# A fused attention, mixture-of-experts and cos-gated MLP kernel: first decay rows through TensorE, a merged score visit, V products in two visits, another last block

## The chip, the cores and the metric

The kernel runs on one core of one Trainium2 chip. The metric is the device time of one execution in microseconds (us); lower is better. Names used below: PE is TensorE (PEld its weight loads), DVE is VectorE, ACT is ScalarE, POOL is GpSimd, SP is SyncE, which here only issues DMAs.

## The reference

Three stages follow one another. With 4 batches, 8 heads, 576 positions and 64 channels a head:

```
s_pos  = max(s, 0);  cum = cumsum(s_pos)
scores = q k^T / 8 + min(-(cum_i - cum_j), 0), causal
attn   = softmax(scores) (row sum + 1e-9);  out = attn @ v          # -> x, 2304 x 512
logits = (x/|x|) (e/|e|)^T / tau;  each token goes to its best of 8 experts
y      = gate * (relu(x @ w1[e]) @ w2[e])                           # 512 -> 1024 -> 512
h      = y @ w_in;  out = (h * cos(h)) @ w_out                      # 512 -> 2048 -> 512
```

## The kernel before

**Attention** (`attention`, lines 67 to 442) works through 16 pairs of heads. A pair's 576 queries are cut into five tiles: tile 4 is the last 64 queries of both heads together, tiles 3, 2, 1 and 0 are 128 queries each and see 512, 384, 256 and 128 keys. `steps` (L205) is the list of all (pair, tile), in the order 4, 3, 2, 1, 0. For one step:

- `emit_s` writes the scores q k^T into two PSUM banks of the pool `ps_s` (four banks), by fp32 products of 64 by 64 (L218 for tile 4, L225 for the others); a tile other than 4 has one bank for each head.
- `emit_m` adds the causal mask to the diagonal block by a bf16 product with the identity `idb` (L235, L238).
- `emit_x` lets DVE add the decay row `c_t` and take the row minimum in one instruction (L255, with a small read-out `mx`), and ACT take the exponential and the row sum (L260).
- `emit_t` transposes the result on PE (L271, L277, banks of `ps_t`) and copies it to `PT` on DVE (tiles 1 and 2) or ACT.
- `av` multiplies by V (L293) once all tiles of a pair are there: 256 query columns first, then 320 (the last pair the other way round).

The loop (L421 to L439) runs at step n: mask of n+3, transposes of n, one turn of the waiting tasks, reductions and exponentials of n+2, scores of n+4, another turn of the tasks. A task is a generator and gives up its turn at each `yield`; `av`, `setup` and, for each batch of four pairs, `rows` and `route` (output rows, router logits, positions, scatter) are such tasks. The order on PE and on SP is the order of this text; DVE, ACT and POOL are ordered by the scheduler of the framework.

`c_t` of a pair holds the running sums of two heads, each spread over 128 partitions, and a third row set for tile 4. The sums are scanned on DVE (L120), written to device memory (`cumd`, L121) and read back with one row for all partitions (L98, L100). `load`, `load_c` and `load_v` of pair p+2 are issued on SP at pair p's first step; `q`, `k` and `c` have three buffers each. `setup` also issues eight writes of zeros over `xr` (L202), 768 KB each.

**Experts** (`moe1`) and **MLP** (`moe2`, lines 812 to 904) follow. The MLP cuts 2304 tokens into blocks of 256 (block 0) and four times 512, and the hidden 2048 into 16 chunks whose weights pass through a ring of six. A window is a run of up to four chunks for one block; its products accumulate in PSUM (`facc`) and are added to `oacc` at its end (L885); where a window ends at chunk 15 the finished rows are scattered to the output by POOL (L887), one instruction for each 128 tokens. `first` (L830) sets after how many chunks a block's first window ends; windows are sorted by end and start.

Of the kernel before, what the change touches and what calls it, by code (L numbers as in the profile page):

```python
# [66 lines left out]
def attention(g, qd, kd, vd, sd, ied, embt, tau, ident, maskd, trid):  # L67
    tc, nc, const, dram, xr = g.tc, g.nc, g.const, g.dram, g.xr
    with ExitStack() as st:
# [25 lines left out]
        def load_c(p, eng=nc.sync):  # L95

            c_t = ct[p] = ld.tile([128, 3, S], F32, tag="c", name="c_t")
            eng.dma_start(out=c_t[:, 0:2], in_=cumd[2 * p:2 * p + 2].unsqueeze(0).to_broadcast([128, 2, S]))  # L98
            for h in range(2):
                eng.dma_start(out=c_t[64 * h:64 * h + 64, 2], in_=cumd[2 * p + h].unsqueeze(0).to_broadcast([64, S]))  # L100
# [7 lines left out]
        mk_f = one.tile([128, 192], F32, name="mk_f")  # L108
        mk_b = one.tile([128, 192], BF16, name="mk_b")
# [97 lines left out]
        sc, px, rs, ot = {}, {}, {}, {}  # L207

        def emit_s(n):
            p, i = steps[n]  # L210
            q0, q1 = QT[i]
            q_t, k_t = qt[p], kt[p]
            if i == 4:
# [6 lines left out]
            else:  # L220
                ts = [ps_s.tile([128, 512], F32, tag="s", name="s_ps") for h in range(2)]
                for u in range(2):
                    for h, t in enumerate(ts):
                        a = q0 + 64 * u
                        nc.tensor.matmul(out=t[64 * u:64 * u + 64, 0:q1], lhsT=q_t[64 * h:64 * h + 64, a:a + 64], rhs=k_t[64 * h:64 * h + 64, 0, 0:q1],  # L225
                                         start=True, stop=False)
                sc[n] = ts

        def emit_m(n):

            p, i = steps[n]
            q0, q1 = QT[i]
            if i == 4:
                t, c0, c1 = sc[n][1]
                nc.tensor.matmul(out=t[:, 224:288], lhsT=idb, rhs=mk_b[:, 128:192], start=False, stop=True)  # L235
            else:
                for t in sc[n]:
                    nc.tensor.matmul(out=t[:, q0:q1], lhsT=idb, rhs=mk_b[:, 0:128], start=False, stop=True)  # L238

        def emit_x(n):  # L240
            p, i = steps[n]
            q0, q1 = QT[i]
# [7 lines left out]
            for h, parts in ((2, sp),) if i == 4 else ((h, [(sp[h], 0, q1)]) for h in range(2)):  # L250
                t = sx.tile([128, S], F32, tag="sx", name="s_sb")
                mx = None
                for ps, c0, c1 in parts:
                    mo = sm.tile([128, 1], F32, tag="mx", name="mx", bufs=12)
                    nc.vector.tensor_tensor_reduce(  # L255
                        out=t[:, c0:c1], in0=ps[:, 0:c1 - c0], in1=ct[p][:, h, c0:c1],
                        scale=-0.125, scalar=(1e30 if mx is None else mx), op0=ALU.add, op1=ALU.min, accum_out=mo)
                    mx = mo
                hd = 2 * hp + h % 2
                nc.scalar.activation(out=t[:, 0:q1], in_=t[:, 0:q1], func=ACTF.Exp, scale=-1.0, bias=mx, accum_out=rs[b][:, i, hd:hd + 1])  # L260
                px[n].append(t)

        def emit_t(n):
            p, i = steps[n]
            q0, q1 = QT[i]
            pt = PT[p % 2]
            w = min(i + 1, 4)
            for h, t in enumerate(px.pop(n)):
                tp = ps_t.tile([128, 4, 128], F32, tag="t", name="t_ps")
                for j in range(w):  # L270
                    nc.tensor.transpose(tp[:, j, :], t[:, 128 * j:128 * j + 128], idt)  # L271
                if i < 4:
                    eng = nc.vector.tensor_copy if i in (1, 2) else nc.scalar.copy
                    eng(out=pt[:, h, 0:w, q0:q1], in_=tp[:, 0:w, :])
                else:
                    tq = ps_t.tile([128, 512], F32, tag="t", name="t_ps")
                    nc.tensor.transpose(tq[0:64, 0:128], t[:, 512:576], idt)  # L277
                    nc.scalar.copy(out=pt[:, :, :, q0:q1].rearrange("p h j q -> p j h q"), in_=tp.rearrange("p j (h q) -> p j h q", h=2))
                    nc.vector.tensor_copy(out=PE4[p % 2], in_=tq[0:64, 0:128].rearrange("p (h q) -> p h q", h=2))

        def av(p):
# [5 lines left out]
            for c0, c1, last in (halves if p + 1 < NPAIR else halves[::-1]):  # L287
                o = ps_o.tile([128, 512], F32, tag="o", name="o_ps")
                for j in range(last + 1):
# [5 lines left out]
                    if j == 1 and j < last:  # L295
                        yield
# [117 lines left out]
        LS, LX = 4, 2  # L414
        for n in range(LS):
# [4 lines left out]
        tasks, starts = [], {3: setup()}  # L420
        for n in range(NS):  # L421
            p, i = steps[n]
            if i == 4 and p + 2 < NPAIR:
# [11 lines left out]
            if i == 0:  # L435
                starts[n + 1] = av(p)
# [375 lines left out]
def moe2(g, wf):  # L812
    tc, nc, const, out = g.tc, g.nc, g.const, g.out
    with ExitStack() as st:
# [15 lines left out]
        first = {1: 1, 2: 2, 0: 3, 3: 4, 4: 4}  # L830
# [6 lines left out]
        windows.sort(key=lambda w: (w[2], w[1]))  # L837
# [69 lines left out]
def host(inputs):  # L907
# [16 lines left out]
    mask = np.zeros((128, 192), np.float32)  # L924
    mask[:, 0:128] = np.where(np.arange(128)[None, :] > np.arange(128)[:, None], np.float32(-8e9), np.float32(0))
    mask[:, 128:] = np.where(np.arange(64)[None, :] > np.arange(128)[:, None] % 64, np.float32(-8e9), np.float32(0))
# [28 lines left out]
```

## Time and profile before

| | us |
|---|---|
| median of three runs | 904.14 |
| lowest, highest | 903.5, 904.35 |
| the profiled execution | 904.9 |
| its span in the profile | 903.1 |
| attention, to the first output-row product of the last batch | 0 to 222.85 |
| experts and MLP, first transposes to last product | 247.34 to 888.95 |
| last scatter of the output starts | 892.75 |

The profile gives the busy time of each engine, the chain of work that ended last, the same instructions in order of time, and the busy time in stretches that one chooses. 1.8 us of the profiled execution lie outside its span. All times in the text are us from the start of the span.

### The profile page before, as it was taken

How to read it: one execution, taken by the hardware profiler on the slowest of the kernel's cores; microseconds unless marked ns; L12 is line 12 of the kernel's file. 1: busy time of each engine (PE TensorE's matmuls, PEld its weight loads, DVE VectorE, ACT ScalarE, POOL GpSimd, SP SyncE). 2: the span in 40 equal slices, each digit the busy share in tenths (PEclk: the TensorE clock that was granted, in tenths of full speed). 3: DMA queues.
4: the chain of work that ended last, by engine and by line, in shares of the span. 5: the costliest groups of instructions: out<-in, count | busy, mean ns of one | idle time of the engine just before them, and what ended most of it. 6: DMA issues, size and time to landing. Idle time of an engine off the chain costs nothing.

```text
span 903.1 us, 14595 instructions
## 1 busy us (share of the span) xinstructions
PE 853.5 (95%) x5289; PEld 682.4 (76%) x5289; DVE 579.7 (64%) x1402; ACT 430.4 (48%) x914; POOL 98.2 (11%) x108
## 2 busy tenths in 40 slices
PE   3999999999199999999999999999999999999993
PEld 1556555565199999999998888888888888888882
DVE  2666767585566656556579986786777847644453
ACT  1766765675255445545554644444334434434330
POOL 0000502204540010111100000000000000000114
PEclk9999999999699999999999999999999999999997
DMA  7989555701484576878654221111011200000113
GB/s 220 248 283 325 179 159 170 234 2 54 134 268 139 150 153 142 178 171 186 160 170 123 84 94 46 48 47 47 24 47 47 71 1 1 0 1 1 47 47 119
DMA packets 40975, 104.30 MB, mean 115 GB/s; under 512 B 8922, under 2 KB 9306, under 8 KB 40898
## 3 DMA queue, kind: packets, MB, share of 16 engines
q1 hardware_dynamic: 36993, 92.90, 36.4%
q0 software_dynamic: 3552, 9.45, 2.8%
q10 hardware_dynamic: 352, 0.96, 0.5%
q8 instruction: 44, 0.72, 0.3%
q14 instruction: 34, 0.27, 0.1%
HBM read 87.48 MB, written 15.81 MB: 114 GB/s over the span
## 4 chain that ended last, share of the span: by engine, by line
PE 89%; DMA 4%; DVE 4%; issue 1%; POOL 0%; SPq 0%; ACT 0%; ACTq 0%; POOLq 0%; DVEq 0%
PE h_ps L856 7%; PE h_ps L857 7%; PE facc L875 7%; PE facc L877 7%; PE facc L876 7%; PE h_ps L855 7%; PE o_ps L293 5%; PE s_ps L225 5%; PE t_ps L271 5%; PE acc L638 4%; PE h_ps L611 4%; PE acc L640 4%; PE acc L639 4%; PE h_ps L613 4%; PE h_ps L612 4%; PE r_ps L327 2%
## 5 line engine op out<-in xcount | busy, mean ns | idle before, releaser
L571 DVE TENSOR_TENSOR wl<-wraw,wh 128x1024 fp32r<-128x1024 f32 x64 | 78.3, 1225 | 84.0 <-ACT wh L569 84.0
L856 PE MATMUL h_ps<-x2l,wh 128*128 128x512 f32 (+1 forms) x320 | 119.0, 372 | 0.2 <-DVE x2l L646 0.2
L857 PE MATMUL h_ps<-x2h,wl 128*128 128x512 f32 (+1 forms) x320 | 118.8, 371 | 0.0
L855 PE MATMUL h_ps<-x2h,wh 128*128 128x512 f32 (+1 forms) x320 | 118.2, 371 | 0.0
L875 PE MATMUL facc<-wh,gh 128*128 128x512 f32 x288 | 114.5, 397 | 0.0
L876 PE MATMUL facc<-wl,gh 128*128 128x512 f32 x288 | 113.9, 395 | 0.0
L877 PE MATMUL facc<-wh,gl 128*128 128x512 f32 x288 | 113.4, 396 | 0.0
L260 ACT ACTIVATE s_sb<-s_sb,mx 128x576 f32<-128x576 f32 (+2 forms) x144 | 83.4, 582 | 49.2 <-DVE mx L255 46.9
L716 ACT ACTIVATE ki<-h_ps 128x512 int32<-128x512 f32 (+1 forms) x80 | 44.4, 555 | 115.1 <-PE h_ps L857 115.1
L569 ACT CAST wh<-wraw 128x1024 fp32r<-128x1024 f32 x64 | 67.2, 1049 | 65.0 <-PE acc L639 54.1
L717 DVE SCALAR_TENSOR_TENSOR ki<-ki,h_ps 128x512 f32<-128x512 int32 (+1 forms) x80 | 50.5, 631 | 70.4 <-ACT ki L716 69.7
L255 DVE CUSTOM_DVE_ANT_0 s_sb<-s_ps,c_t 128x288 f32<-128x288 f32 (+2 forms) x144 | 65.3, 481 | 38.9 <-DMA c_t<-cumd 11.4
L611 PE MATMUL h_ps<-xth,wh 128*128 128x384 f32 (+7 forms) x256 | 78.6, 308 | 0.5 <-ACT xth L597 0.3
L639 PE MATMUL acc<-hl,wh 128*128 128x384 f32 (+7 forms) x256 | 78.4, 306 | 0.4 <-DVE hl L617 0.4
L718 ACT ACTIVATE ki<-ki,hpi 128x512 f32<-128x512 f32 (+1 forms) x80 | 54.6, 683 | 50.5 <-DVE ki L717 50.1
L638 PE MATMUL acc<-hh,wh 128*128 128x384 f32 (+7 forms) x256 | 78.4, 308 | 0.0
L640 PE MATMUL acc<-hh,wl 128*128 128x384 f32 (+7 forms) x256 | 78.3, 306 | 0.0
L613 PE MATMUL h_ps<-xth,wl 128*128 128x384 f32 (+7 forms) x256 | 77.6, 304 | 0.1
L612 PE MATMUL h_ps<-xtl,wh 128*128 128x384 f32 (+7 forms) x256 | 77.6, 304 | 0.0
L856 PEld LDWEIGHTS h_ps<-x2l,wh 128*128 128x128 f32 x320 | 60.1, 188 | 12.5 <-issue 0.4
L855 PEld LDWEIGHTS h_ps<-x2h,wh 128*128 128x128 f32 x320 | 60.0, 188 | 12.6 <-issue 0.2
L862 ACT CAST gh<-ki 128x512 fp32r<-128x512 f32 (+1 forms) x80 | 46.3, 578 | 48.2 <-DVE ki L719 48.2
(182 smaller groups left out, 1645.6 us busy)
## 6 DMA issues: line engine op xcount, KB each, us to landing
wraw<-in_wcat_dram SPq DMA_DIRECT2D x64, 512.0 KB, 4.4
wraw<-in_wf_dram SPq DMA_DIRECT2D x32, 512.0 KB, 3.4
c_t<-cumd SPq DMA_DIRECT2D x15, 576.0 KB, 7.7
xr<-zr SPq DMA_DIRECT2D x8, 768.0 KB, 5.6
v_t<-in_vd_dram SPq DMA_DIRECT2D x16, 320.0 KB, 5.7
q_t<-in_qd_dram SPq DMA_DIRECT2D x16, 288.0 KB, 3.2
k_t<-in_kd_dram SPq DMA_DIRECT2D x16, 288.0 KB, 3.8
c_t<-cumd SPq DMA_DIRECT2D x30, 144.0 KB, 5.9
```

The costliest lines, as they stand in the source:

```text
L611: nc.tensor.matmul(out=ps[:, 0:c], lhsT=wh[:, sl], rhs=th[:, k, 0:c], start=(k == 0), stop=False)
L612: nc.tensor.matmul(out=ps[:, 0:c], lhsT=wh[:, sl], rhs=tl[:, k, 0:c], start=False, stop=False)
L613: nc.tensor.matmul(out=ps[:, 0:c], lhsT=wl[:, sl], rhs=th[:, k, 0:c], start=False, stop=(k == 3))
L638: nc.tensor.matmul(out=ps[:, 0:c], lhsT=wh[:, sl], rhs=hh[:, 0:c], start=(f == 0), stop=False)
L639: nc.tensor.matmul(out=ps[:, 0:c], lhsT=wh[:, sl], rhs=hl[:, 0:c], start=False, stop=False)
L640: nc.tensor.matmul(out=ps[:, 0:c], lhsT=wl[:, sl], rhs=hh[:, 0:c], start=False, stop=(f == 7))
L855: nc.tensor.matmul(out=ps[:, 0:w], lhsT=wh[:, sl], rhs=g.x2h[:, k, a0:a1], start=(k == 0), stop=False)
L856: nc.tensor.matmul(out=ps[:, 0:w], lhsT=wh[:, sl], rhs=g.x2l[:, k, a0:a1], start=False, stop=False)
L857: nc.tensor.matmul(out=ps[:, 0:w], lhsT=wl[:, sl], rhs=g.x2h[:, k, a0:a1], start=False, stop=(k == 3))
L875: nc.tensor.matmul(out=acc[t], lhsT=gh[:, sl], rhs=wh[:, 512:1024], start=(c == s), stop=False)
L876: nc.tensor.matmul(out=acc[t], lhsT=gh[:, sl], rhs=wl[:, 512:1024], start=False, stop=False)
L877: nc.tensor.matmul(out=acc[t], lhsT=gl[:, sl], rhs=wh[:, 512:1024], start=False, stop=(c == e))
```

## The change

Five things are changed.

1. The decay rows of pair 0 no longer come from device memory. `first_c` multiplies the 32 scanned rows on PE by a 32 x 128 selection matrix (a column of the identity, repeated; `sel2` for the tile-4 rows), six fp32 products of 288 columns, and copies each from PSUM, three on ACT and three on DVE. `cumd` is still written, for the other pairs. The identity is loaded ahead of pair 0's q and k.
2. Tiles 1 and 0 become one step. Its two banks first take a 384-column bf16 product with a wider mask (zeros, then two causal blocks), and the scores of both tiles accumulate onto it; reductions and exponentials stay apart, six transposes go to two banks. A pair has four steps in place of five.
3. The `yield` within the 320-column half of `av` is gone: all its products stand together.
4. `setup` starts at step 2 in place of 3 and waits 8 turns in place of 20.
5. In the MLP block 3 has its first window end where block 0 had it, and block 0 where block 4 has it; the sort puts block 0's window behind all others that end at chunk 15. Block 0 so ends alone, with four chunks; before it ended last with one.

```diff
+        nc.sync.dma_start(out=idt, in_=ident)
         load(0)
-        nc.sync.dma_start(out=idt, in_=ident)
         nc.sync.dma_start(out=mk_f, in_=maskd)
...
         nc.scalar.dma_start(out=cumd, in_=cum)
-        load_c(0, nc.scalar)
         nc.vector.tensor_copy(out=idb, in_=idt)
         nc.vector.tensor_copy(out=mk_b, in_=mk_f)
+
+        ct[0] = ld.tile([128, 3, S], F32, tag="c", name="c_t")
+        sel2 = one.tile([B * H, 128], F32, name="sel2")
+        nc.vector.tensor_copy(out=sel2.rearrange("p (a b) -> p a b", a=2), in_=idt[0:B * H, 0:2].unsqueeze(2).to_broadcast([B * H, 2, 64]))
+
+        def first_c(k):
+            sel = sel2 if k == 2 else idt[0:B * H, k:k + 1].to_broadcast([B * H, 128])
+            for c0, eng in ((0, nc.scalar.copy), (288, nc.vector.tensor_copy)):
+                ps = ps_t.tile([128, 512], F32, tag="t", name="c_ps")[:, 0:288]
+                nc.tensor.matmul(out=ps, lhsT=sel, rhs=cum[:, c0:c0 + 288], start=True, stop=True)
+                eng(out=ct[0][:, k, c0:c0 + 288], in_=ps)
...
-            for _ in range(20):
+            for _ in range(8):
                 yield
...
-        steps = [(p, i) for p in range(NPAIR) for i in (4, 3, 2, 1, 0)]
+        TILES = ((4,), (3,), (2,), (1, 0))
+        steps = [(p, t) for p in range(NPAIR) for t in TILES]
...
+            ts = [ps_s.tile([128, 512], F32, tag="s", name="s_ps") for h in range(2)]
+            two = len(tiles) == 2
+            if two:
+                for t in ts:
+                    nc.tensor.matmul(out=t[:, 0:384], lhsT=idb, rhs=mk_b[:, 0:384], start=True, stop=False)
+            for i, (q0, q1), o in places(tiles):
                 for u in range(2):
                     for h, t in enumerate(ts):
                         a = q0 + 64 * u
-                        nc.tensor.matmul(out=t[64 * u:64 * u + 64, 0:q1], lhsT=q_t[64 * h:64 * h + 64, a:a + 64], rhs=k_t[64 * h:64 * h + 64, 0, 0:q1],
-                                         start=True, stop=False)
-                sc[n] = ts
+                        nc.tensor.matmul(out=t[64 * u:64 * u + 64, o:o + q1], lhsT=q_t[64 * h:64 * h + 64, a:a + 64], rhs=k_t[64 * h:64 * h + 64, 0, 0:q1],
+                                         start=not two, stop=two and i == 0)
...
-                    if j == 1 and j < last:
-                        yield
...
+        first_c(2)
         for n in range(LS):
             emit_s(n)
             emit_m(n)
             if n < LX:
                 emit_x(n)
-        tasks, starts = [], {3: setup()}
+            if n == 0:
+                first_c(0)
+                first_c(1)
+        tasks, starts = [], {2: setup()}
...
-        first = {1: 1, 2: 2, 0: 3, 3: 4, 4: 4}
+        first = {1: 1, 2: 2, 3: 3, 4: 4, 0: 4}
...
-        windows.sort(key=lambda w: (w[2], w[1]))
+        windows.sort(key=lambda w: (w[2], w[2] == 15 and w[0] == 0, w[1]))
...
-    mask = np.zeros((128, 192), np.float32)
+    mask = np.zeros((128, 448), np.float32)
```

What this moves on the engines, at three places. PE at the start of the program, before:

```order
L218 MATMUL s_ps<-k_t,q_t 64x288 [waits DMAHW2_49,DMAHW1_49]
L218 MATMUL s_ps<-k_t,q_t 64x288 [waits DMAHW4_49,DMAHW3_49]
L218 MATMUL s_ps<-k_t,q_t 64x288 x2
L235 LDWEIGHTS idb [waits DVE_49]
L235 MATMUL s_ps<-mk_b,idb 128x64 [waits DVE_49]
L225 MATMUL s_ps<-k_t,q_t 64x512 x4
```

and in the changed kernel (`sel_121` is `sel2`):

```order
L133 MATMUL c_ps<-cum,sel_121 128x288 [waits DVE_49]
L133 MATMUL c_ps<-cum,sel_121 128x288
L234 MATMUL s_ps<-k_t,q_t 64x288 [waits DMAHW3_49,DMAHW2_49]
L234 MATMUL s_ps<-k_t,q_t 64x288 [waits DMAHW5_49,DMAHW4_49]
L234 MATMUL s_ps<-k_t,q_t 64x288 x2
L253 LDWEIGHTS idb
L253 MATMUL s_ps<-mk_b,idb 128x64 [waits DVE_49]
L133 MATMUL c_ps<-cum,idt 128x288 [waits DMAHW1_49]
L133 MATMUL c_ps<-cum,idt 128x288 [waits DVE_49] x2
L133 MATMUL c_ps<-cum,idt 128x288 [waits Activation_49]
L246 MATMUL s_ps<-k_t,q_t 64x512 x4
```

Six products stand ahead of tile 3's scores, two of them ahead of all others; the wait is for DVE, not for a load of `c_t`. PE within one pair, the scores of tiles 2 and 1 of the next pair between the transposes of this one, before:

```order
L225 MATMUL s_ps<-k_t,q_t 64x384 x4
L238 LDWEIGHTS idb
L238 MATMUL s_ps<-mk_b,idb 128x128
L238 LDWEIGHTS idb
L238 MATMUL s_ps<-mk_b,idb 128x128
L271 MATMUL t_ps<-idt,s_sb 128x128 [waits DVE_49,Activation_49] x2
L225 MATMUL s_ps<-k_t,q_t 64x256
L225 MATMUL s_ps<-k_t,q_t 64x256 [waits DVE_49]
L225 MATMUL s_ps<-k_t,q_t 64x256 x2
```

and in the changed kernel:

```order
L257 MATMUL s_ps<-mk_b,idb 128x128
L288 MATMUL t_ps<-idt,s_sb 128x128 [waits Activation_49]
L288 MATMUL t_ps<-idt,s_sb 128x128 x2
L288 MATMUL t_ps<-idt,s_sb 128x128 [waits DVE_49]
L288 MATMUL t_ps<-idt,s_sb 128x128 x2
L241 LDWEIGHTS idb
L241 MATMUL s_ps<-mk_b,idb 128x384
L241 LDWEIGHTS idb
L241 MATMUL s_ps<-mk_b,idb 128x384 [waits DVE_49]
L246 MATMUL s_ps<-k_t,q_t 64x256 x4
L246 MATMUL s_ps<-k_t,q_t 64x128 x4
```

Six transposes now stand ahead of the products that need the banks of the 512-key tile, where two stood, and the 128-key scores follow at once. PE at the end of the MLP, before (the last block's two accumulators are `facc_9289` and `facc_9293`):

```order
L877 MATMUL facc_9265<-wh,gl 128x512
L875 MATMUL facc_9289<-wh,gh 128x512
L876 MATMUL facc_9289<-wl,gh 128x512
L877 MATMUL facc_9289<-wh,gl 128x512
L875 MATMUL facc_9293<-wh,gh 128x512
L876 MATMUL facc_9293<-wl,gh 128x512
L877 MATMUL facc_9293<-wh,gl 128x512
```

and in the changed kernel, the last three chunks of block 0 (`facc_9142`, `facc_9146`) behind the products that feed them:

```order
L877 MATMUL h_ps<-x2h,wl 128x256
L895 MATMUL facc_9142<-wh,gh 128x512
L896 MATMUL facc_9142<-wl,gh 128x512
L897 MATMUL facc_9142<-wh,gl 128x512
L895 MATMUL facc_9146<-wh,gh 128x512
L896 MATMUL facc_9146<-wl,gh 128x512
L897 MATMUL facc_9146<-wh,gl 128x512
L895 MATMUL facc_9142<-wh,gh 128x512
L896 MATMUL facc_9142<-wl,gh 128x512
L897 MATMUL facc_9142<-wh,gl 128x512
```

The last 512-token block is now followed by two whole chunks of block 0 with their hidden products, and two more output products, where one chunk's six products followed it.

## Rows read from the trace of the kernel before

**Rows 1.** The page: busy time, and chain by engine.

```profile
PE 853.5 (95%) x5289; PEld 682.4 (76%) x5289; DVE 579.7 (64%) x1402; ACT 430.4 (48%) x914; POOL 98.2 (11%) x108
PE 89%; DMA 4%; DVE 4%; issue 1%; POOL 0%; SPq 0%; ACT 0%; ACTq 0%; POOLq 0%; DVEq 0%
```

**Rows 2.** Chain of work at the start: start us, us, what.

```profile
4.52 3.85 DMA cumd<-cum
...
9.38 9.16 DMA c_t<-cumd
...
24.24 0.64 PE s_ps L225 x8
...
27.46 0.14 PE s_ps L235
```

**Rows 3.** Timeline, start: start us, us, engine, line, operation, shapes, [idle before].

```profile
8.69 1.98 PE L225 MATMUL s_ps<-k_t,q_t 64*64 64x512 f32 x8
...
18.72 0.46 DVE L255 CUSTOM_DVE_ANT_0 s_sb<-s_ps,c_t 128x288 f32<-128x288 f32 x1 [11.43 <-DMA c_t<-cumd]
```

**Rows 4.** Chain of work through one pair without output rows.

```profile
110.44 1.12 PE s_ps L218 x8
...
112.78 0.14 PE s_ps L235
112.92 0.69 PE t_ps L271 x6
...
114.88 0.86 PE s_ps L225 x6
115.74 0.22 PE s_ps L238 x2
...
116.40 0.81 PE s_ps L225 x8
...
117.65 1.07 PE s_ps L225 x8
...
119.49 0.38 PE s_ps L225 x8
```

**Rows 5.** Timeline of the pair before that one, around tile 1's scores.

```profile
104.70 0.69 DVE L255 CUSTOM_DVE_ANT_0 s_sb<-s_ps,c_t 128x512 f32<-128x512 f32 x1 [1.53 <-PE s_ps L238]
...
105.32 0.75 DVE L274 COPY pt<-t_ps 128x256 f32<-128x256 f32 x2
...
106.73 0.20 PEld L225 LDWEIGHTS s_ps<-k_t,q_t 64*64 64x64 f32 x6 [0.20 <-DVE mx L255]
```

**Rows 6.** Stretches: us, busy PE PEld DVE ACT POOL (count), PE clock, DMA share, GB/s.

```profile
0.00:20.00 20.00, 6.45 (x24) 1.98 (x27) 4.57 (x18) 0.07 (x1) 1.74 (x22) 1.00 0.71 199
65.00:70.00 5.00, 5.00 (x51) 3.06 (x49) 3.90 (x18) 4.97 (x17) 0.00 (x0) 1.00 1.03 396
108.54:119.87 11.33, 11.33 (x104) 5.97 (x106) 6.55 (x27) 7.80 (x26) 3.48 (x4) 1.00 0.71 233
119.87:136.05 16.18, 15.77 (x134) 10.13 (x136) 10.83 (x45) 11.02 (x36) 0.11 (x1) 1.00 0.41 123
```

**Rows 7.** Timeline of the end of the MLP: its last products and scatters.

```profile
881.64 0.28 PE L857 MATMUL h_ps<-x2h,wl 128*128 128x256 f32 x1
...
884.51 0.42 DVE L863 TENSOR_TENSOR gl<-ki,gh 128x256 fp32r<-128x256 f32 x1 [0.47 <-ACT gh L862]
...
887.59 2.10 DVE L885 TENSOR_TENSOR oacc<-facc,oacc 128x512 f32<-128x512 f32 x3
...
888.33 0.40 PE L876 MATMUL facc<-wl,gh 128*128 128x512 f32 x1
888.56 0.39 PE L877 MATMUL facc<-wh,gl 128*128 128x512 f32 x1
...
892.75 0.96 POOL L887 DMA_INDIRECT out_dram<-oacc,ti  x1 [0.30 <-DMA out_dram<-oacc,ti]
```

**Rows 8.** Timeline of the DMA queue on SP: writes of zeros.

```profile
63.36 5.84 SPq L202 DMA_DIRECT2D xr<-zr  x5
```

More of the change, by code (lines that the diff above doesn't have):

```diff
@@ L107, in attention @@
         nc.sync.dma_start(out=s_t, in_=sd)
-        mk_f = one.tile([128, 192], F32, name="mk_f")
-        mk_b = one.tile([128, 192], BF16, name="mk_b")
+        mk_f = one.tile([128, 448], F32, name="mk_f")
+        mk_b = one.tile([128, 448], BF16, name="mk_b")
         idt = g.idt = const.tile([128, 128], F32, name="idt")
         idb = one.tile([128, 128], BF16, name="idb")
+        nc.sync.dma_start(out=idt, in_=ident)
         load(0)
-        nc.sync.dma_start(out=idt, in_=ident)
         nc.sync.dma_start(out=mk_f, in_=maskd)
@@ L202, in setup, with places @@
                 nc.sync.dma_start(out=xr[e * NT:e * NT + 384].rearrange("(p c) d -> p c d", p=128), in_=zr.unsqueeze(1).to_broadcast([128, 3, DM]))
-        steps = [(p, i) for p in range(NPAIR) for i in (4, 3, 2, 1, 0)]
+        TILES = ((4,), (3,), (2,), (1, 0))
+        steps = [(p, t) for p in range(NPAIR) for t in TILES]
         NS = len(steps)
         sc, px, rs, ot = {}, {}, {}, {}
+        def places(tiles):
+            return [(i, QT[i], 256 if len(tiles) == 2 and i == 0 else 0) for i in tiles]
         def emit_s(n):
-            p, i = steps[n]
-            q0, q1 = QT[i]
+            p, tiles = steps[n]
             q_t, k_t = qt[p], kt[p]
-            if i == 4:
+            if tiles == (4,):
                 sc[n] = []
@@ L219, in emit_s @@
                     sc[n].append((t, c0, c1))
-            else:
-                ts = [ps_s.tile([128, 512], F32, tag="s", name="s_ps") for h in range(2)]
+                return
+            ts = [ps_s.tile([128, 512], F32, tag="s", name="s_ps") for h in range(2)]
[4 more added lines that the diff above has]
+            for i, (q0, q1), o in places(tiles):
                 for u in range(2):
@@ L248, in emit_x @@
             sp = sc.pop(n)
-            for h, parts in ((2, sp),) if i == 4 else ((h, [(sp[h], 0, q1)]) for h in range(2)):
+            for h in (2,) if tiles == (4,) else range(2):
                 t = sx.tile([128, S], F32, tag="sx", name="s_sb")
[L252 to L260, printed above, removed]
-                px[n].append(t)
+                px[n].append(t)
+                for i, (q0, q1), o in places(tiles):
+                    mx = None
+                    for ps, c0, c1 in sp if h == 2 else [(sp[h], 0, q1)]:
+                        mo = sm.tile([128, 1], F32, tag="mx", name="mx", bufs=12)
+                        nc.vector.tensor_tensor_reduce(
+                            out=t[:, o + c0:o + c1], in0=ps[:, o:o + c1 - c0], in1=ct[p][:, h, c0:c1],
+                            scale=-0.125, scalar=(1e30 if mx is None else mx), op0=ALU.add, op1=ALU.min, accum_out=mo)
+                        mx = mo
+                    hd = 2 * hp + h % 2
+                    nc.scalar.activation(out=t[:, o:o + q1], in_=t[:, o:o + q1], func=ACTF.Exp, scale=-1.0, bias=mx, accum_out=rs[b][:, i, hd:hd + 1])
@@ L263, in emit_t @@
         def emit_t(n):
-            p, i = steps[n]
-            q0, q1 = QT[i]
+            p, tiles = steps[n]
             pt = PT[p % 2]
-            w = min(i + 1, 4)
             for h, t in enumerate(px.pop(n)):
                 tp = ps_t.tile([128, 4, 128], F32, tag="t", name="t_ps")
-                for j in range(w):
+                for j in range(4 if tiles == (4,) else sum(i + 1 for i in tiles)):
                     nc.tensor.transpose(tp[:, j, :], t[:, 128 * j:128 * j + 128], idt)
[L272 to L275, printed above, removed]
+                if tiles == (4,):
@@ L281, in av @@
+                for i, (q0, q1), o in places(tiles):
+                    eng = nc.vector.tensor_copy if i in (1, 2) else nc.scalar.copy
+                    eng(out=pt[:, h, 0:i + 1, q0:q1], in_=tp[:, o // 128:o // 128 + i + 1, :])
         def av(p):
@@ L419, in attention @@
                 emit_x(n)
-        tasks, starts = [], {3: setup()}
+            if n == 0:
+                first_c(0)
+                first_c(1)
+        tasks, starts = [], {2: setup()}
         for n in range(NS):
-            p, i = steps[n]
-            if i == 4 and p + 2 < NPAIR:
+            p, tiles = steps[n]
+            if tiles == (4,) and p + 2 < NPAIR:
                 load(p + 2)
@@ L434, in attention @@
                 emit_s(n + LS)
-            if i == 0:
+            if tiles == TILES[-1]:
                 starts[n + 1] = av(p)
```

30 lines of the change are left out of this document (15 added, 15 removed).

## The prediction

> **What bounds the kernel now.** I read the page first. PE is busy 95% of the span and carries 89% of the chain that ended last [rows 1], so a change pays where it shortens PE's own work or where PE stands still. Three places were then read closely.
>
> *The start.* The chain of waits: the running sums go into device memory at 4.52 (3.85), come back with one row for all partitions (9.16, to 18.54) [rows 2], and only at 18.72 does the first reduction begin, after DVE was idle for 11.43. PE had the scores of tiles 4 and 3 done at 8.69+1.98=10.67 [rows 3]; it is busy for 6.45 of the first 20 us [rows 6].
>
> *The pair.* From one pair's first V products to the next pair's, 108.54 to 119.87, PE is busy for all 11.33, DVE for 6.55, ACT for 7.80 [rows 6]. But one piece is too long for its columns. A visit of scores takes 0.38 for 128 keys, 0.81 for 384, and 0.86 and a little for 512; tile 1 with 256 keys takes 1.07 [rows 4]. On the line from 0.38 to 0.9 (1.36 ns a column, some 0.2 fixed) it should be 0.55. The timeline of the pair before names the other 0.5: there PE's weight loads stand until DVE has reduced the second half of the 512-key tile, whose bank these scores take; the first reduction (0.69) and two copies (0.75) came ahead of it on DVE [rows 5]. So the busy figure hides a wait.
>
> *The end.* The last product ends at 888.56+0.39=888.95, the last scatter at 892.75+0.96=893.71, 4.76 later; scatters follow each other every 0.96+0.30=1.26 [rows 7], and six stand behind the last 512-token block (four of its own, two of block 0).
>
> The sums are made against the profiled execution, 904.9, of which 1.8 lie outside the span of 903.1. The median is 904.14, 0.08% less; I subtract the sum from the median.
>
> **Part 1, the first pair: gains 8.5, bounds 5.5 to 9.7.** I walk PE to one state: all scores of pair 0, transposes of its tiles 4 and 3, pair 1's tile 4 with mask. Before, that is reached at 27.46+0.14=27.60 [rows 2]. Early visits are slow: 512 keys take 1.98 [rows 3] against 0.9 later, and 128 keys still 0.64 at 24.24 [rows 2] against 0.38 [rows 4], although the granted clock reads 1.00 over the first 20 us [rows 6]. So I use the early rate, 1.98/512 = 3.87 ns a column of keys, for the scores up to there.
>
> A decay product (32 rows, 288 columns, to 128 partitions) has no row. By the transposes (0.69 for six of 128 columns, 0.9 ns a column [rows 4]) it takes 0.26 later and, by 1.98/0.9, 0.57 early; by the tile-4 visit, where 2x288 columns take 1.12 [rows 4], 0.56 and 1.2. I take 0.55 and 1.1, nearest to the row with the same columns and type. In order: sums 4.5, selection columns ready 4.95, two decay products 7.1, scores of tile 4 (576 columns x 3.87 = 2.2) 9.3, mask 9.55. Tile 4's reduction needs no more than these, and starts before 10. Four decay products (two early, two late: 3.4) 12.9; 512 keys 0.9, mask 0.2, 384 keys 0.8, mask 0.2: 15.0. The merged visit waits for two 512-key reductions (2x0.69 [rows 5], from 14.1), 15.5, then takes 0.3+0.6: 16.4. Tile 4's transposes 0.55, pair 1's tile 4 and mask 1.12+0.14, tile 3's transposes 8x0.115=0.9: 19.1. The gain is 27.6-19.1=8.5. With decay products at the cheap end 1.2 more; if every visit to the end runs at the early rate, 3 less. The three copies on ACT put its first exponential at about 13, for which nobody on this walk waits. Pair 1's `c_t` still goes through memory. Before, write and read took 13 with pair 0's reads in the same queues; these are gone, so it is there by about 18, and wanted at 17.6 to 19.6.
>
> **Part 2, the pair from then on: gains 8.2, bounds 3 to 11.** Only what changes [rows 4]. Scores of tiles 1 and 0, 1.07+0.38=1.45, become one visit of 0.2 fixed and 384 columns x 1.36, some 0.75. Their masks, two of 0.22, become one of 2x384 columns: bf16 columns cost (0.22-0.14)/192 = 0.4 ns (a mask of 64 columns against two of 128), so 0.06 fixed and more for 768 columns: 0.37 to 0.45; no gain. V loses one visit, 0.1. That is 0.7+0.1=0.8 of 11.33; I take 0.75, so 10.55 to 10.6. Some 0.5 of it is the wait.
>
> Does the wait go? The merged visit still needs the banks of the 512-key tile. Behind that tile's mask, before, PE had four transposes (0.46), 0.81, 0.22 and two transposes (0.23) = 1.72 to do; now the two are six (0.69): 2.18. DVE needs two reductions and the copies: 2x0.69+0.75=2.13 with the order of [rows 5]. It just fits; up to 0.2 may stay, and what is queued behind it on PE are the scores of tiles 1 and 0 and the next pair's V products. What is late next: tile 3 of the pair after must wait until four reductions of the merged tile have read two banks. By 0.69 for 512 columns [rows 5] and 0.46 for 288 [rows 3] they take 2x(0.43+0.30)=1.5 and their read-outs; over 4 us of PE's work (0.92+1.12+V's half+0.14+0.69) lie between.
>
> Eight pairs have no output rows: 8x0.75=6.0. Three times two pairs share PE with them; the first of such two takes 16.18 with PE busy for 15.77 [rows 6], so a wait is covered there in part: 0.5 for each two, 1.6. Pair 0's rest 0.6. Total 8.2. The lower bound is 0.24 a pair (only two visits' fixed part); the upper one 0.75 in all of fifteen.
>
> Here a rule speaks. One mask of 64 columns takes 0.14, two of 128 take 0.22 [rows 4]: some 0.1 of a visit does not grow with columns, and a pair has 12 changes of product form in place of 14. The Trainium skill, "TensorEngine Tiling (Array Packing)", § Key Properties, says that a change of the tiling mode, and not merely of the tile, drains TensorE. The row's 0.1 agrees. By the rule 2x0.1 a pair is won through merging alone; without it only the wait, and the total would be about 6.
>
> **Part 3, the end: gains 2.3, bounds 1 to 2.8.** Products of 512 columns start 0.23 apart [rows 7], so a chunk's six take 1.40, and its twelve hidden ones of 256 columns as much. Between the last 512-token block's last product and PE's end now stand two hidden and four output chunks: 8.4. The block's four scatters, 4x1.26=5.1, are over by then. The first of block 0's two accumulators is complete 0.7 before PE's end, so its addition (2.10/3=0.70 [rows 7]) ends with it; two scatters of 1.26 follow: PE's end + 2.5 in place of 4.76. A 256-token chunk's chain from its last hidden product (881.64+0.28) to `gl` (884.51+0.42) takes 3.0 [rows 7]; 2.8 of output products cover it, so up to 0.5 may be lost: the lower bound with one scatter late.
>
> **Edits costed at nothing.** The eight writes of zeros move some 15 us earlier, into SP's queue in groups between the loads of `q`, `k`, `c` and `v`. Before, five took 5.84 to issue [rows 8], and DMA behind them was at 1.03 share and 396 GB/s [rows 6]. 6.3 MB at that rate are 16 us; loads are issued two pairs ahead, and I estimate their delay at 3 to 4 of the 10 us in hand. If that cover is gone, PE waits 4 to 8 for `q`, `k` or `c`. The turn of V is in the pair's sum. In the MLP the same products run; the other order of blocks costs 0 to +-1.
>
> **The rivals.** *The wait only moves*: DVE is as late for the merged visit and a pair stays at 11.3. For it: 2.13 against 2.18 is no margin. Against it: DVE has 4.8 of 11.33 free, and copies can pass behind the reduction. 904.1-8.5-2.3=893.3. The Trainium skill, "Perfetto Trace Analysis", § Identifying the Most-Contended Engine, holds matmul busy time a poor measure and wants the share of weight loads; that is 5.97/11.33=53% here [rows 6], and agrees with a wait that hides in a full PE. *All at the good end*: 9.7+11+2.6=23.3, 880.8. *Loads late* behind the zeros: 4 to 8 lost, 890 to 894. *Slower*: the merged tile holds its two banks so long that PE waits 2.3 for its four reductions in each pair; the pair becomes 10.55+2.3=12.85, 15x1.52=22.8 lost against 10.8 won, 916. It decides from 10.8/15=0.72 over 11.33, a pair of 12.05. Against it: the 4 us of cover. *No change*: for the start if the decay products stood behind a load of `c_t`, which their order excludes, and for the pair if the first rival holds; both and a lost end give 904.
>
> **How the numbers follow.** 8.5+8.2+2.3=19.0; I leave 0.9 for the 0.2 that may stay in some pairs and the 0.5 at the end: 18.1, so 904.1-18.1 = 886.0. Chances: this case (883 to 889.5) 0.58, the wait moves 0.20, all good 0.10, loads late 0.05, no change 0.03, slower 0.04. The range 880.5 to 894.5 takes in the good end, the moved wait and late loads. 0.2% (1.8) is about what a measurement of this kernel tells from no change. Faster 0.93, same 0.03, slower 0.04.
>
> **What would show it.** Part 1: first reduction before 11, pair 1's tile-4 mask near 18; wrong if that stands at 22 or later. Part 2: a pair near 10.55 with no weight load of the merged visit released by DVE; 11.3 with such a wait is the first rival, above 12 the slower one. Part 3: the last scatter ends 2.4 to 3 behind the last product. Cover: no PE wait for `q_t`, `k_t` or `c_t` from 30 to 80. The forecast falls if early PE keeps its slow rate far beyond 26, or if pairs with output rows get longer.

## The result and the profile after

The changed kernel takes 891.21 us (median of 4 runs, 890.66 to 897.09) where the kernel before takes 904.25 (4 runs): a ratio of 0.9869 with an interval of 0.9827 to 0.9912, 13.0 us less. The forecast was 886.0, 18.1 less, with a range of 880.5 to 894.5. The sign and the range held; five of the 18 us are missing. The experiments show that two terms were too high by 4.6 and 5.0 us and others too low.

The profiled execution took 891.58, its span 889.7 against 903.1. Where these 13.4 went, by the timelines of PE and POOL:

| from ... to | before | after | gain | forecast |
|---|---|---|---|---|
| 0 to the state of the walk (pair 0's scores, pair 1's tile 4 and mask, two transposed tiles) | 27.60 | 23.67 | 3.9 | 8.5 |
| on to the first output-row product of the last batch | 195.1 | 189.4 | 5.7 | 8.2 |
| on to the first expert rows | 24.6 | 24.8 | -0.2 | 0 |
| experts and MLP, to the last product's end | 641.6 | 640.6 | 1.0 | 0 |
| on to the end of the span | 14.2 | 11.1 | 3.0 | 2.3 |

The page of after, engines (compare [rows 1]):

```profile
PE 851.1 (96%) x5269; PEld 685.9 (77%) x5269; DVE 578.8 (65%) x1408; ACT 431.8 (49%) x917; POOL 98.0 (11%) x108
```

PE works only 2.4 us less than before; the rest of the gain is time in which it no longer stands still, or that lay behind its last product.

The timeline of the start of after (start us, us, engine, line, operation, shapes, count, [idle before]), which answers to [rows 2, 3]. L133 are the decay products, L246 the scores:

```profile
4.77 2.28 PE L133 MATMUL c_ps<-cum,sel 32*128 32x288 f32 x4 [4.77 <-DVE sel L127]
...
9.71 2.28 PE L133 MATMUL c_ps<-cum,idt 32*128 32x288 f32 x4
...
12.40 0.45 DVE L275 CUSTOM_DVE_ANT_0 s_sb<-s_ps,c_t 128x288 f32<-128x288 f32 x1
...
12.54 2.28 PE L133 MATMUL c_ps<-cum,idt 32*128 32x288 f32 x4 [0.55 <-DVE c_t L134]
14.76 1.99 PE L246 MATMUL s_ps<-k_t,q_t 64*64 64x512 f32 x8
...
17.00 1.56 PE L246 MATMUL s_ps<-k_t,q_t 64*64 64x384 f32 x8
...
22.67 1.07 PE L288 MATMUL t_ps<-idt,s_sb 128*128 128x128 f32 x8
```

PE starts at 4.77 and does not stop again but for 0.55, so the wait of [rows 2] is gone. But it is busy at the slow rate: each two decay products take 2.28 all three times, and the scores of 512 and 384 keys 1.99 and 1.56, not 0.9 and 0.8.

Stretches of after (us; busy time and count of PE, PEld, DVE, ACT, POOL; clock; DMA), one pair without output rows and two pairs with them. They answer to [rows 6]:

```profile
102.36:113.08 10.72, 10.72 (x101) 6.13 (x100) 6.33 (x29) 7.56 (x25) 6.67 (x7) 1.00 0.91 290
62.53:91.33 28.80, 28.14 (x244) 17.72 (x243) 19.33 (x82) 18.77 (x57) 0.94 (x3) 1.00 0.73 237
```

A pair is 10.72 long where it was 11.33. Of the lists of waits, two lines matter: of before, from 30 to 205, the weight loads in the scores (total us, times, longest), and of after PE in the merged mask:

```profile
PEld s_ps L225 <- DVE mx L255: 3.5, 12, 0.4
```

```profile
PE s_ps L241 <- DVE lw L350: 1.4, 3, 0.5
```

The wait of the 256-key scores for DVE's reductions, twelve times before, is not in the list of after, neither for PE nor for its weight loads. A new one is: three times, where output rows are made, the merged visit waits for DVE's `lw`, the last reader of an output-row bank.

The tail of after, which answers to [rows 7]:

```profile
871.65 0.38 ACT L736 ACTIVATE ki<-h_ps 128x256 int32<-128x256 f32 x1 [1.66 <-PE h_ps L877]
...
878.18 0.39 PE L897 MATMUL facc<-wh,gl 128*128 128x512 f32 x1
...
880.14 0.96 POOL L907 DMA_INDIRECT out_dram<-oacc,ti  x1 [0.30 <-POOLq L748]
```

The last scatter ends at 881.10, 2.53 behind the last product's end at 878.57; before it was 4.76.

### The profile page after: what moved, and what is told of

Its sections match the earlier page's. It is cut to its first block, busy times and chain, and to the rows that moved or that the text cites. A ratio compares the mean times of both kernels' runs of the same rounds, so it can differ in the third digit from the quotient of the medians.

```text
span 889.7 us, 14464 instructions
## 1 busy us (share of the span) xinstructions
PE 851.1 (96%) x5269; PEld 685.9 (77%) x5269; DVE 578.8 (65%) x1408; ACT 431.8 (49%) x917; POOL 98.0 (11%) x108
```

## Experiments

Twelve runs followed, in three groups of four; two of them repeat a kernel that had run. Each group ran on one chip, beside the kernel before. The chips differ: the kernel before had medians of 905.01, 905.46 and 903.64 there. So times are compared within a group, and each ratio is to the kernel before of its group, with its interval. The stretch "from the state on" is that of the table's second line, "state" its first.

### First group: each part alone, and PE at work before the start

Start alone, on the kernel before:

```diff
+        nc.sync.dma_start(out=idt, in_=ident)
         load(0)
-        nc.sync.dma_start(out=idt, in_=ident)
...
-        load_c(0, nc.scalar)
...
+        first_c(2)
         for n in range(LS):
             emit_s(n)
...
+            if n == 0:
+                first_c(0)
+                first_c(1)
```

> The kernel before with the new start alone (decay rows of pair 0 through PE, identity loaded first). Theory A, the parts add up and each is worth what the two traces show: the score visit of pair 1's tile 4 began 26.28 before and 21.51 after, so 4.8 less, about 899.5. Theory B, the forecast's price of the start: 8.5 less, 895.7. Rival C, pairs of five steps can't use the earlier start because their scores wait for DVE: under 2 less, above 902.

Measured: 901.70, 3.3 less, ratio 0.9961 (0.9943 to 0.9980). In its trace pair 1's tile 4 begins at 21.64 and the output rows of the last batch at 218.18, 4.5 earlier than before; from the state on nothing changes (195.3). Theory A was nearest, a little dear; B, the forecast's 8.5, is refuted.

Merged tiles alone:

```diff
-        steps = [(p, i) for p in range(NPAIR) for i in (4, 3, 2, 1, 0)]
+        TILES = ((4,), (3,), (2,), (1, 0))
+        steps = [(p, t) for p in range(NPAIR) for t in TILES]
...
```

> The kernel before with tiles 1 and 0 in one visit alone (five-step pairs become four-step pairs; start, V's turn, the zeros and the MLP's order as before). Theory A, from the traces: attention up to the last output rows is 9.6 shorter in the changed kernel, 4.8 of it the start, so 4.8 less here, about 899.5, a normal pair near 10.8. Theory B, the forecast: 8.2 less, 896. Rival C, V's turn must go too for the wait to vanish: pair 11.1 or more, 2 to 3 less, about 901.5.

Measured: 894.28, 10.7 less, ratio 0.9885 (0.9860 to 0.9910). That is more than any theory gave, and as much as nearly the whole change. From the state on its trace has 185.9 against 195.1 before and 189.4 in the changed kernel. So the changed kernel holds something that takes back 3.5. The two-pair stretch with output rows of this kernel, under that of after above:

```profile
62.44:90.28 27.84, 27.71 (x243) 17.17 (x242) 20.72 (x89) 18.93 (x60) 0.32 (x3) 1.00 1.01 337
```

It is 27.84 long, with PE idle for 0.13, against 28.80 and 0.66. Its start puzzled: pair 1's tile 4 began at 21.63 although pair 0's rows still came from device memory. Its first reduction says why, they had landed early (15.78, not 18.72):

```profile
15.78 0.46 DVE L264 CUSTOM_DVE_ANT_0 s_sb<-s_ps,c_t 128x288 f32<-128x288 f32 x1 [6.92 <-DMA c_t<-cumd]
```

The MLP's order alone:

```diff
-        first = {1: 1, 2: 2, 0: 3, 3: 4, 4: 4}
+        first = {1: 1, 2: 2, 3: 3, 4: 4, 0: 4}
...
-        windows.sort(key=lambda w: (w[2], w[1]))
+        windows.sort(key=lambda w: (w[2], w[2] == 15 and w[0] == 0, w[1]))
```

> The kernel before with the MLP's order of last windows alone. Theory A, from the traces: 2.2 less between the last product and the last scatter, 0.8 less behind it, and 1.0 less in experts and MLP, 900.2 in all. Theory B, the forecast: 2.3 less, 901.9. Rival C: the 1.0 in the MLP comes from elsewhere: 901.2.

Measured: 902.94, 2.1 less, ratio 0.9988 (0.9969 to 1.0006); the interval reaches 1, so this alone settles no more than that it is small. The trace has 2.52 between the last product's end and the last scatter's, as in the changed kernel. Theory B is nearest; A's 4.0 lies outside the interval.

Products on zeros ahead of the first decay product, on the changed kernel:

```diff
+        wz = one.tile([128, 512], BF16, name="wz")
+        nc.vector.memset(wz, 0.0)
+        w_ps = ps_o.tile([128, 512], F32, tag="o", name="w_ps")
+        for _ in range(9):
+            nc.tensor.matmul(out=w_ps, lhsT=wz[:, 0:128], rhs=wz, start=True, stop=True)
```

> The changed kernel with nine bf16 products of 128x512 on zeros ahead of the first decay product, which fill PE from about 1.3 to the arrival of the running sums; their results are not used. Theory W, the early products are slow because PE stood idle before: with PE at work earlier they become fast earlier, 512-key scores take 0.9 instead of 2.0 or change over well before 20.3, the visit of pair 1's tile 4 begins before 18 instead of 21.5, and the time is 3 to 6 below the changed kernel, 885 to 888. Rival D, they are slow because of something else at the start (the loads keep the DMA engines at a share of 1.0 until 30): nothing changes, 891.

Measured: 894.49, ratio 0.9886 (0.9862 to 0.9910), to be set beside 0.9869 and 0.9876 for the changed kernel itself: no gain. The stretches and two products of its start:

```profile
8.00:10.00 2.00, 2.00 (x7) 0.93 (x5) 0.60 (x3) 0.00 (x0) 0.00 (x0) 0.50 1.07 288
10.00:17.00 7.00, 6.45 (x22) 2.42 (x24) 2.19 (x7) 1.56 (x4) 0.00 (x0) 0.50 1.04 313
```

```profile
4.79 1.23 PE L138 MATMUL c_ps<-cum,sel 32*128 32x288 f32 x4
...
12.05 2.28 PE L138 MATMUL c_ps<-cum,idt 32*128 32x288 f32 x4 [0.55 <-DVE c_t L139]
14.27 1.98 PE L251 MATMUL s_ps<-k_t,q_t 64*64 64x512 f32 x8
```

This is the most telling trace of the study. The first two decay products, right behind the nine, take 1.23, the price I had called "late". Then, between 7 and 8, the granted clock falls to 0.50, its lower level of 1.2 GHz, and the same products take 2.28 and the 512-key scores 1.98: to a hundredth what they take in the kernels without the nine products, where the same column reads 1.00. So those ran at the lower level too, and the 1.00 of [rows 6] for 0 to 20 is no reading of it. Neither theory held whole. Of theory W, two of six decay products became fast, and pair 1's tile 4 began at 19.90, not before 18 (21.51 and 20.49 in the two traces of the changed kernel). Theory D has the time right, but not its reason: in the third group the 512-key scores take 1.09 with the DMA engines at a share of 1.0 and more (16 to 20).

### Second group: V's turn, the zeros, the start

The changed kernel again:

> The changed kernel again, as the measure for the three beside it. All theories: 891, first reduction near 10, attention up to the last output rows 213.1, a two-pair stretch with output rows 28.8.

Measured: 894.11, ratio 0.9876 (0.9858 to 0.9894), 11.4 less. Pair 1's tile 4 at 20.49, 189.8 from the state on.

V's products in two turns again:

```diff
                     for h in range(2):
                         nc.tensor.matmul(out=o[64 * h:64 * h + 64, a - c0:c1 - c0], ...
+                    if j == 1 and j < last:
+                        yield
```

> The changed kernel with V's 320-column products again in two turns (the rest as changed). Theory Y, taking the turn away lost time: output rows came one turn earlier and their banks and DVE work stood ahead of the merged visit, 28.8 against 27.84 for two pairs with output rows where the turn is kept, three times, and about 0.15 in the other pairs. Then 2.5 to 3.5 less than the changed kernel. Theory F, the forecast: one visit more a pair, 0.1 each, 1.5 more.

Measured: 890.76, ratio 0.9847 (0.9820 to 0.9874), 3.4 less than the changed kernel beside it. Theory Y holds. Its stretches:

```profile
51.60:62.32 10.72, 10.72 (x102) 5.92 (x101) 6.71 (x29) 8.08 (x26) 0.00 (x0) 1.00 1.04 360
62.32:90.16 27.84, 27.71 (x244) 17.18 (x243) 19.79 (x83) 18.92 (x60) 0.33 (x3) 1.00 0.85 262
```

A pair without output rows is 10.72 with one V visit more: the visit that I priced at 0.1 costs nothing there. Two pairs with output rows are 0.96 shorter. How, is seen in the timelines. Of the changed kernel:

```profile
69.95 0.76 PE L343 MATMUL r_ps<-ie,ot 128*128 128x144 f32 x4
70.64 1.21 PE L246 MATMUL s_ps<-k_t,q_t 64*64 64x384 f32 x8
71.78 0.76 PE L343 MATMUL r_ps<-ie,ot 128*128 128x144 f32 x4
...
73.15 0.66 PE L343 MATMUL r_ps<-ie,ot 128*128 128x144 f32 x4
73.64 0.33 PE L241 MATMUL s_ps<-mk_b,idb 128*128 128x384 bf16 x1
74.44 0.34 PE L241 MATMUL s_ps<-mk_b,idb 128*128 128x384 bf16 x1 [0.48 <-DVE lw L350]
```

and with the turn kept:

```profile
69.58 0.81 PE L246 MATMUL s_ps<-k_t,q_t 64*64 64x384 f32 x6
...
70.53 0.76 PE L345 MATMUL r_ps<-ie,ot 128*128 128x144 f32 x4
...
71.90 0.66 PE L345 MATMUL r_ps<-ie,ot 128*128 128x144 f32 x4
72.39 0.49 PE L241 MATMUL s_ps<-mk_b,idb 128*128 128x384 bf16 x2
```

L343 and L345 are the output rows; each line is one group, with a bank of its own. Each turn of the tasks places what comes next on PE. With one turn less, three groups stand ahead of the merged visit, the first of them ahead of the 384-key scores; the banks are from the four that the scores use, and DVE is behind with reading them. The scores then take 1.21 instead of the 0.88 of other pairs, and the second half of the merged mask waits 0.48 for the reading of the third group. With the turn kept, two groups stand there, both behind the 384-key scores, and the merged mask runs through. From the state on: 185.7 against 189.8. Three times 0.96, 2.9 of these 4.1, lie in the pairs with output rows.

Setup as before as well:

```diff
-        tasks, starts = [], {2: setup()}
+        tasks, starts = [], {3: setup()}
...
-            for _ in range(8):
+            for _ in range(20):
```

> The changed kernel with V's turn kept and with setup as before (from step 3, 20 turns). Theory A: the earlier zeros are worth nothing, the same as the run with the turn alone within 0.7. Rival L: the earlier zeros delay loads, then this one is 1 or more faster than it.

Measured: 889.81, ratio 0.9829 (0.9813 to 0.9845). The medians are 0.95 apart, but from the state on both traces have 185.7, and 0.64 of the difference is there before any zero is written (23.20 against 23.84). The earlier zeros are worth nothing, and they do no harm; theory A.

The merged visit and the MLP's order on the kernel before, without the decay products:

> The kernel before with the merged visit and the MLP's order of last windows: no decay rows through PE, V's turn kept, setup as before; it differs from the run above in the start alone. Theory S, the decay rows through PE are worth nothing once the tiles are merged: pair 1's tile 4 at 21.6 with or without, so the same time as the run above within 0.7, about 3 under the changed kernel. Rival P, that agreement came from loads of pair 0's rows that happened to land at 15.8 instead of 18.5: then this run has its first reduction at 18 to 19 and loses 2.5 to 3 against the run above.

Measured: 893.54, ratio 0.9863 (0.9844 to 0.9882), 3.7 slower than the run above, from which it differs in the start alone. Rival P holds: without the luck of the first group's load the first reduction is at 18.01.

```profile
18.01 0.46 DVE L264 CUSTOM_DVE_ANT_0 s_sb<-s_ps,c_t 128x288 f32<-128x288 f32 x1 [9.86 <-DMA c_t<-cumd]
```

Its state is reached at 26.85, against 23.20. So the decay products are worth 3.7 with merged tiles as well, and merging itself 0.6 to 0.8 at the start.

### Third group: the clock, and the end

The measure is the best kernel so far, V's turn kept and setup as before.

> The changed kernel with V's turn kept and setup as before, again, as the measure for the three beside it. All theories: 890, attention up to the last output rows about 209, pair 1's tile 4 between 20.5 and 21.7.

Measured: 889.07, ratio 0.9839 (0.9826 to 0.9853).

With the nine products and decay products over all 128 rows:

```diff
...
-        cum = sx.tile([128, S], F32, tag="sx", name="cum")[0:B * H]
+        cum4 = sx.tile([128, S], F32, tag="sx", name="cum")
+        nc.gpsimd.memset(cum4, 0.0)
+        cum = cum4[0:B * H]
...
-                nc.tensor.matmul(out=ps, lhsT=sel, rhs=cum[:, c0:c0 + 288], start=True, stop=True)
+                nc.tensor.matmul(out=ps, lhsT=sel, rhs=cum4[:, c0:c0 + 288], start=True, stop=True)
...
```

> The same with nine idle-time products of 128x512 ahead of the first decay product, and the decay products over 128 rows of which 96 are zero. Theory W: the early products are slow because PE's clock is at its lower level there, whatever the row says without such products; with PE at work from 1.2 and full-height decay products it stays at the upper level, 512-key scores take 1.0 instead of 2.0, and pair 1's tile 4 begins at 14 to 17 instead of 21: 3 to 6 less. Rival D: the clock falls again as in the run with the nine products alone (0.50 from 8 to 17), pair 1's tile 4 stays at 19.5 to 21 and the gain is under 1.5.

Measured: 890.97, ratio 0.9862 (0.9847 to 0.9877), 1.9 slower; its four times all lie above the measure's five. The run is spoiled as a test of time: the first decay product began at 9.50 instead of 4.8. The zeros were written by 2.00, but DVE's order now has the running sums behind the cast of the mask, which waited for its load:

```profile
7.44 0.39 DVE L130 CAST mk_b<-mk_f 128x448 bf16<-128x448 f32 x1 [4.01 <-DMA mk_f<-in_maskd_dram]
...
8.10 1.34 DVE L127 TENSOR_TENSOR_SCAN cum<-z_t,s_t 32x576 f32<-32x576 f32 x1
```

PE in the same trace:

```profile
9.50 2.29 PE L140 MATMUL c_ps<-cum,sel 128*128 128x288 f32 x4 [4.90 <-DVE cum L127]
...
13.88 3.97 PE L140 MATMUL c_ps<-cum,idt 128*128 128x288 f32 x8
17.78 1.09 PE L253 MATMUL s_ps<-k_t,q_t 64*64 64x512 f32 x8
```

Yet pair 1's tile 4 begins only 1.25 later (22.29 against 21.04). The clock had fallen during the wait of 4.90 (1.00 to 7, 0.63 from 7 to 8, then 0.50) and comes back as the last decay product ends (0.75 from 17 to 18, then 1.00), and the 512-key scores take 1.09. Theory D's fall of the clock came. Whether such products could hold the clock from the start was not shown.

Fifty products while PE waits for the expert rows:

```diff
-        nc.tensor.matmul(out=cp, lhsT=g.ones_b, rhs=g.cacc)
+        ins = nc.tensor.matmul(out=cp, lhsT=g.ones_b, rhs=g.cacc)
+        w_ps = ps_t.tile([128, 512], F32, tag="t", name="w_ps")
+        with tc.issue_after(ins.ins):
+            for _ in range(50):
+                tc.keep_in_program_order(nc.tensor.matmul(out=w_ps, lhsT=g.ones_b, rhs=g.ones_b.unsqueeze(1).to_broadcast([128, 4, 128]), start=True, stop=True))
```

> The same as the measure with 50 products of 128x512 on constants in the 15 us in which PE waits for the expert rows; their results are not used. Theory W: the granted clock reads 0.50 when the first expert rows arrive, transposes and hidden products take twice their later time until 238; with the products it reads 1.00 and 1.5 to 2.5 are won. Rival R: the products are still running when the rows arrive, or take what they give: 0 or up to 2 lost.

Measured: 890.41, ratio 0.9855 (0.9840 to 0.9870): 1.3 above the measure, intervals overlapping. The fillers ran as meant and ended 3.66 before the rows came:

```profile
218.37 12.64 PE L490 MATMUL w_ps<-ones_b 128*128 128x512 bf16 x50
234.66 1.27 PE L622 MATMUL xt_ps<-idt,xw 128*128 128x128 f32 x6 [3.66 <-DMA xw<-xr]
236.08 0.66 PE L637 MATMUL h_ps<-xth,wh 128*128 128x384 f32 x1
```

Two stretches from the moment when they came:

```profile
234.00:236.00 2.00, 1.21 (x6) 0.62 (x6) 0.00 (x0) 0.50 (x2) 2.00 (x1) 0.88 0.97 355
236.00:238.00 2.00, 1.92 (x7) 1.59 (x8) 1.15 (x3) 1.66 (x3) 2.00 (x2) 0.50 0.95 360
```

The granted clock was still 1.00 when the rows arrived at 234.66 (the 0.88 is 1.00 up to 235.5 and 0.5 behind it), and the first six transposes took 1.27 instead of 1.52. So it fell with the transposes running; the hidden product at 236 takes 0.66, as it does without the fillers. The rows also came 0.8 later, counted from the output rows; why, the runs do not show. The time is in rival R's range, if for another reason than the one I gave.

The old order of the MLP's last windows in the measure:

> The same as the measure with the MLP's last windows in the old order. Theory T: block 0 at the end wins 2.2 between the last product and the last scatter and 0.7 behind it, and gives back the 1.3 to 1.6 that PE waits for block 0's cosines in the newer traces: this run is 1.3 to 1.6 slower than the measure. Theory B, the forecast: 2.3 slower. Rival N: the waits eat the gain, the same within 0.5.

Measured: 890.27, ratio 0.9854 (0.9839 to 0.9869), 1.2 slower than the measure. The intervals overlap; the four times lie above the measure's five, the nearest by 0.05. Theory T is nearest. The ends of the two traces, first the old order, then the new:

```profile
874.29 0.39 PE L899 MATMUL facc<-wh,gl 128*128 128x512 f32 x1
878.51 0.96 POOL L909 DMA_INDIRECT out_dram<-oacc,ti  x1 [0.30 <-DMA out_dram<-oacc,ti]
```

```profile
876.45 0.40 PE L899 MATMUL facc<-wh,gl 128*128 128x512 f32 x1
878.42 0.96 POOL L909 DMA_INDIRECT out_dram<-oacc,ti  x1 [0.30 <-POOLq L750]
```

In the new order the last scatter follows sooner, as forecast, but the last product is 2.2 later, so the scatter ends at the same time; the span is 0.8 shorter for what lies behind it. PE's wait for block 0's cosines is 1.3 of the 2.2; what the other 0.9 is was not settled.

## Why the prediction was right, and where not

*The start (8.5 forecast, 3.9 measured).* The mechanism was right: the trip through device memory is off the path, and PE works from 4.77. Up to the first mask the walk is exact (9.55 forecast, the mask ends at 9.77 in the trace). The step that failed is the one that gave the visits behind it their later rates: "Four decay products (two early, two late: 3.4)", "512 keys 0.9", "384 keys 0.8". They took 5.1 with a wait of 0.55, 2.0 and 1.6, and the merged visit was slow as well: of the 4.6 that are missing, 1.9 lie in the decay products, 1.8 in the scores and masks of 512 and 384 keys and 0.7 in the merged visit. I had a bound ("if every visit to the end runs at the early rate, 3 less") and chose the other end, with no row for when the slow rate would stop. The bound itself was summed too small: by the same early rates the visits up to the merged one alone make 3.3 (1.1 for two decay products, 1.1, 0.7 and 0.9 for the three visits of scores, less a wait of 0.5), and the visits behind it nearly 3 more. So the gain could fall 1.6 below it although the slow rate ended at about 20.8. Behind it stood the reading of 1.00 for the clock, which hid that the slow rate is the clock's lower level. One check of mine misfired: the first reduction came at 12.40, not before 11, since DVE had the next copy of a decay product ahead of it. PE waited 0.55 for that copy, and not for the reduction.

*The pair (8.2 forecast, 5.7 measured).* Two errors of opposite sign. Merging the tiles alone gave 9.2 from the state on (195.1 to 185.9), more than the 6.7 that are left of my 8.2 when V's 0.1 in each of fifteen pairs is taken out. The pairs with output rows make the difference: 1.6 for each two, three times 29.44 to 27.84, where I had 0.5. The wait for the 512-key bank went as argued. Removing V's turn, counted as a gain of 0.1 a pair, cost 3.7 to 4.1. The failed step is "V loses one visit, 0.1": without output rows the pair is 10.72 either way, so the visit had no price, and the removed turn moved output rows ahead of the merged visit, which I had not followed past the V products. I had asked what is queued behind the merged visit, and not what a turn less puts ahead of it. The forecast's "0.5 for each two" was 0.64 in the trace of the result and is 1.6 with the turn.

*The rule of tiling modes.* The masks and scores of the merged visit took 0.42 and 0.81, near the 0.37 to 0.45 and 0.75 of the forecast. V's joined visit, a change of product form less, shows 0.00 (10.72 with and without). So 0.1 is not the price of every change in this kernel. Nor does the plain pair settle it: of its 0.61 less (11.33 to 10.72) the wait is 0.3 (3.5 in 12 times, on the weight loads) to 0.5 (the forecast's estimate). The Trainium skill, "TensorEngine Tiling (Array Packing)", § Key Properties, has TensorE drained at a change of mode; whether it is drained there and the drain is hidden, no run here shows.

*The end (2.3 forecast, 3.0 in the first trace; run by itself, 2.1 put in and 1.2 taken out).* The scatter's distance came out (2.53 for 2.5, so 2.2 of the 3.0); the other 0.8 lies behind the last scatter and was not forecast. What the distance bought depends on a term that I had at "up to 0.5": the chain of a 256-token block against 2.8 of products. In the profiled execution of the result PE never waited for it. In all nine later traces with the new order it waited, 1.3 to 2.2 in total, because ACT started the first step of a cosine 2.0 to 3.5 us after its input was ready. Same program, two executions; compare the 871.65 with idle 1.66 above:

```profile
873.61 0.39 ACT L736 ACTIVATE ki<-h_ps 128x256 int32<-128x256 f32 x1 [3.69 <-PE facc L897]
...
878.95 0.50 PE L895 MATMUL facc<-wh,gh 128*128 128x512 f32 x1 [1.34 <-ACT gh L882]
```

The input's last product began at 871.20 in that trace. What held ACT stays open; the products named as releaser are not its input. In the old order 512-token products cover such a pause.

*Costed at nothing.* Right for the zeros (185.7 with either setup), and no PE wait for `q_t`, `k_t` or `c_t` came in the trace of the result. The 1.0 that experts and MLP gained in the first trace was not found again. From the output rows to the last product the trace of the result has 665.5, but the nine later traces with the new order have 667.3 to 669.0, and the kernel before and three further traces with the old order 665.8 to 666.5. So as a rule the new order costs 1 to 3 there, the wait for the cosines included, and gives back much of what it wins at the end; "0 to +-1" was too little.

*The rivals.* "The wait only moves" fell for plain pairs, but a kin of it is what happened beside output rows: the new wait of the merged mask for `lw`. None of the others showed.

That the sum fell into its range is in part luck: the start was 4.6 too high and V's turn 5.0 (a gain of 1.5 forecast, a loss of 3.5), against an unforeseen 2.5 more from merging and, in that trace, 1.7 more from the MLP and the end. The version that the experiments point to, the changed kernel with V's turn kept, ran faster than both: 889.81 against 894.11 and 905.46 on one chip (setup as before too, which makes no difference).

## To carry to other kernels

Where work is placed by turns, removing a turn moves everything behind it; follow the next task's first instructions to the banks and engines that they will hold before calling the removal a saving. A step that starts earlier also runs under the rates of that earlier time: price each piece by rows of the time at which it will now stand, and where the rate's change has no row, take the dear end. And a change of several parts that comes out in range should still be run part by part: here one of five was a loss of 3.4 us.

## What the runs showed of the hardware

In the twelve traces without the nine products the granted clock reads 1.00 in every stretch up to 30. With nine products ahead it read 1.00 to 7, 0.70 from 7 to 8 and 0.50 from 8 to 17, and the 512-key scores took 1.98 under 0.50 as they do under that early 1.00; under a 1.00 that follows a change they take 1.09. The nine products say the same: their weight loads start 0.43 apart where the clock reads 1.00 (2.01, 2.44, 2.87 and on), as those of the fifty start where it reads 0.50 (219.13, 219.55, 219.98). An early 1.00 is therefore no sign of the upper level; the durations are.

The clock also fell with PE at work, between 7 and 8 of that trace: ahead of it stand the nine products, two decay products, two products of a score visit and a wait of 0.54.

A PE that had run for 12.64 up to 231 still had the upper level when work came at 234.66, and lost it at 235.5, in the middle of that work.

One load of the same rows, issued at the same place, landed so that the first reduction was at 15.78 in one trace and at 18.01, 18.3 and 18.72 in three others. A single trace of a start that waits for loads can be off by 2 to 3 us, which here made one part look worthless.
